# RWKV mixing and a squared-ReLU FFN on one core: steps moved at four places of a hand-written order

## The chip, the cores and the metric

One Trainium2 chip, one of its cores. The metric is the device time of one launch in microseconds (us), as the median of several runs. Five engines work side by side: PE (TensorE, matrix products), DVE (VectorE), ACT (ScalarE), POOL (GpSimd) and SP (SyncE, here only an issuer of transfers). Each runs its own list of instructions in order and waits by semaphores for what the others write. Matrix products land in PSUM, which has eight banks; operands lie in SBUF.

## The reference

An RWKV time mixing in four batches, eight heads of 48 and 768 time steps feeds a feed-forward block of width 384 and hidden width 2048. All inputs and the output are fp32.

```python
for t in range(S):                       # per batch and head
    y[t]  = r[t] @ (state + (u * k[t])^T v[t])
    state = w^T * state + k[t]^T v[t]
x   = y of all heads side by side        # 3072 x 384
out = square(max(x @ w_in, 0)) @ w_out   # 384 -> 2048 -> 384
```

## The kernel before, in words

**Tiling.** Time is cut into chunks of 128 steps. A unit is one chunk of one batch, 128 rows of x; there are 24, numbered in the order in which they are worked. Inside a chunk the recurrence becomes matrix products. r and k are scaled by decay factors (`rh`, `kh`), transposed, and multiplied to scores (`A`), which a triangular mask cuts (`Bm`). Y is the product of masked scores and v, plus the state's part from the second chunk of a batch on. The term of u is a vector: P0 = r times k, P1 = P0 times u, du = its sum over a head, dv = du times v. The state goes on by `U` (k times v), `ts` (U plus state) and `S` (times decay). Units 0 to 3 are *paired*: two chunks of a batch are loaded together with the time steps de-interleaved, so that even steps are unit 2q and odd ones unit 2q+1. They have steps of their own (`lp`, `TK`, `TR`, `Ap`, `Bp`, `YD`, `YI`, `UP`).

**The FFN** works on groups of units: groups 0 and 1 are units 0 and 1, group 2 is units 2 and 3, then two units each (group 4 is units 6 and 7, group 8 is units 14 and 15), and the last two groups are one unit each. `F1.g.s` is piece s of x times w_in for group g, into one PSUM bank: for a group of one unit four pieces of 12 matmuls of 128 columns, for a group of two eight pieces of 6 matmuls of 256 columns. `re` takes the ReLU out of the bank, `sq` squares it, `F2.i.q` is a quarter of the second product for unit i, `os` copies it out and `out` sends it.

**What sets the order.** The string `ORDER` is a table written by hand, one entry for each step, `name.arguments:engine/slots`, with engines A (ACT), D (DVE), G (POOL), P (PE) and S (SP). Each engine runs its steps in the table's order. The slots name the buffers, for PE's steps the PSUM banks; a step that writes a buffer waits for the last reader of what was in it. The dictionary `HELD` says which buffers a step takes.

The steps that the prediction names, with their lines in the kernel before:

- Loads, on SP: `ld.v.16` (L322) brings v of unit 16, which `vb.16` (a copy to bf16, L252 on ACT and L254 on DVE) reads. W_in comes in four parts (`V`), w_out in four (`W`), both issued on POOL.
- `kh` (L338), `rh` (L341), `P0` (L344), `P1` (L348): products of two SBUF tiles, some on DVE, some on POOL. kh.8 and kh.10 are on POOL, kh.11, P0.8, rh.4 and kh.5 on DVE. `du` is L351, `dv` L356.
- `T` (L399, on PE) transposes r and k of a unit into a bank, `Tc` copies that to SBUF. `XB` does the same by a DMA transpose.
- `Ap` (L385) and `A` (L412): scores. `Bp.q.a.h` (L393) and `Bm.i.h` (L420): masks, on DVE, each out of one bank; a is the parity of the time step, h that of the head.
- `YD.0`: Y of units 0 and 1, 36 matmuls. Four bring in dv by an identity (L429), 32 take the masked scores of both a and both h (L438). `YI` adds the state's part (L449). `Y` (L460, L462) is that of the other units.
- `UP` (L472), `U` (L482); `S0` (L496), `ts` (L499), `S` (L502).
- `xs` (L493 on DVE; a copy at L252 or L254 for units 0 to 3) takes Y out of its bank. Then `X` (L507, transposes on PE) and `xTc` (copy into xT) bring x into the form that F1 (L523) reads, or `xX` (L514) does it by one DMA transpose issued on SP. xTc.14 and xX.15 fill the two halves of the xT that F1.8.7, the first piece of group 8, reads.
- `re` (L533 on ACT, L535 on DVE), `sq` (L540 on ACT, L542 on DVE), `F2` (L551).
- `Z.n` (L583): matmuls of the identity whose result nobody reads; Z.7 is four instructions (one of 512 columns, three of 128) behind UP.0.

Behind Z.7 PE does Ap.1.0, YD.0, YI.1, UP.1, X.0, Ap.1.1, X.1, F1.0.3, F1.1.3 and F1.0.0. F1.0.0 uses the bank of UP.1, which ts.3 empties. F1.4.1 and F1.4.7 are the first two pieces of group 4; F1.4.7 takes the bank of U.7, which ts.7 empties. F1.2.4, F1.2.7 and F1.2.5 are the first three of group 2; F1.2.5 follows F1.1.2 in its bank. F2.1.1 takes the bank of A.4, which the masks of unit 4 empty.

Of the kernel before, what the change touches and what calls it, by code (L numbers as in the profile page):

```python
# [26 lines left out]
lp.v.1:S/1 bc:P/3 P0.1:G/0 Wk.0:A/4 rh.1:D/0 ld.r.5:S/4 Wt.0:A/5 bu:P/6 kh.0:D/1 V.3:G WLcol:A P0.0:D/1 Wk.1:A/7  # L27
rh.0:D/1 TR.0:P/0 ld.k.4:S/4 V.0:G kh.1:D/0 ub:A V.1:G TK.0:P/3 rh.3:D/2 rh.2:D/3 RC.0:A/0 KC.0:A/1 ld.r.4:S/5 P1.0:G
TR.1:P/2 vb.0:A/0 vb.1:A/1 kh.2:D/3 kh.3:D/2 Z.2:P/6 Ap.0.1:P/7/5 Ap.0.0:P/4/0 V.2:G P1.1:D TK.1:P/3 ld.k.5:S/5
du.0:D/0 dv.0:G RC.1:A/2 du.1:D/1 dv.1:G Bp.0.1.1:D/0 UP.0:P/6/5 Bp.0.1.0:D/1 Bp.0.0.1:D/2 KC.1:A/3 vb.3:A/2 WLm:G  # L30
Z.7:P/2 Ap.1.0:P/7/2 vb.2:A/3 Bp.0.0.0:D/3 P0.2:G/2 S0.0:D YD.0:P/0/3 ld.v.4:S/4 P1.2:G ts.1:D/1 xs.0:A/0 YI.1:P
Bp.1.0.1:D/4 UP.1:P/4/6 Bp.1.0.0:D/6 X.0:P/5 xs.1:A/1 xTc.0:D/0 S0.2:D Ap.1.1:P/2/0 X.1:P/3 F1.0.3:P/7 ts.3:D/0
xTc.1:A/1 F1.1.3:P/5 P0.3:G/3 P1.3:G du.2:D/2 re.0.3:D/0 F1.0.0:P/6 Bp.1.1.1:D/5 dv.2:G Wt.2:A re.0.0:A/1 W.1:G
du.3:D/3 ld.v.5:S/5 Wk.2:A F1.1.0:P/4 F1.1.1:P/3 dv.3:G re.1.0:A/2 F1.0.1:P/0 rh.5:G/4 re.1.3:A/3 Bp.1.1.0:D/7
YD.1:P/1/7 YI.3:P sq.1.3:A/0 re.0.1:A/4 W.2:G xs.3:D/2 xs.2:A/3 kh.4:D/5 re.1.1:A/5 sq.1.0:D/1 ld.k.6:S/6 W.3:G
F1.0.2:P/6 X.2:P/4 rh.4:D/5 sq.0.0:A/2 X.3:P/2 F1.1.2:P/5 W.0:G re.0.2:D/3 xTc.3:A/0 sq.0.3:A/3 xTc.2:D/0 re.1.2:A/2
P0.4:D/4 T.4:P/0 Tc.4:D/4 F1.2.4:P/1 F1.2.7:P/4 sq.1.2:D/4 F1.2.5:P/5 re.2.4:D/1 re.2.7:A/0 ld.r.6:S/6 sq.0.2:A/5
# [9 lines left out]
F2.2.3:P/4 ld.r.11:S/2 ts.6:D/1 F2.2.1:P/4 sq.3.3:D/17 P0.9:G/3 sq.3.0:A/18 ld.r.10:S/3 F2.2.0:P/4 sq.3.6:A/19  # L47
F1.3.7:P/0 os.2:D/3 du.6:D/2 A.7:P/5/6 A.6:P/1/2 ld.k.11:S/2 re.3.7:A/2 vb.7:G/7 F1.3.5:P/4 Bm.7.1:D/0 sq.3.2:A/20
rh.8:G/2 F2.4.0:P/0 ld.k.10:S/3 Bm.7.0:D/1 Bm.6.0:D/2 Bm.6.1:D/3 sq.3.7:A/21 rh.9:G/1 S.3:G F2.4.1:P/0 re.3.5:D/1
ld.v.8:S/0 XB.9:S/0 P1.9:D dv.6:G out.2:S F2.4.3:P/0 rh.11:G/3 F2.5.0:P/6 ld.v.9:S/1 P0.8:D/4 sq.3.4:A/22 Y.6:P/5  # L50
rh.10:G/5 ld.r.13:S/5 sq.3.5:A/23 F2.5.3:P/6 xs.6:D/1 Y.7:P/4 X.6:P/5 kh.8:G/2 F2.5.1:P/6 xs.7:D/2 xTc.6:A/2 kh.11:D/3
X.7:P/4 U.7:P/5 kh.10:G/5 F2.4.2:P/0 xTc.7:A/2 ts.7:D/0 XB.11:S/2 vb.8:A/0 F1.4.1:P/4 os.4:A/4 S.7:D F1.4.7:P/5
re.4.1:A/3 P0.10:D/1 du.9:D/3 XB.8:S/3 U.8:P/0 F2.5.2:P/6 re.4.7:A/4 vb.9:G/1 S.6:D F1.4.3:P/4 os.5:A/5 XB.10:S/4
P1.8:D re.4.3:D/0 F1.4.4:P/5 F1.4.0:P/6 re.4.4:A/2 rh.13:D/4 ld.k.13:S/4 F1.4.2:P/4 ts.8:D/0 ld.v.11:S/2 re.4.0:A/5
# [17 lines left out]
re.6.4:A/2 xs.12:D/2 xX.12:S/2 F2.11.0:P/2 os.9:D/1 sq.6.4:A/21 P0.16:G/0 XB.17:S/3 ts.13:D/1 Y.13:P/1 kh.16:D/5  # L72
F2.10.3:P/6 rh.16:G/5 F2.10.2:P/6 xs.13:D/3 out.5:S du.15:D/4 ld.k.18:S/4 F2.10.0:P/6 P1.16:G ld.r.21:S/3 A.15:P/7/5
A.14:P/0/3 ld.r.19:S/2 Bm.15.0:D/5 dv.15:G F2.11.1:P/2 ld.r.18:S/5 Bm.15.1:D/7 S.13:G X.13:P/7 F2.11.3:P/2 xTc.13:A/2
Bm.14.0:D/4 Y.15:P/5 vb.14:G/7 du.14:D/0 F1.7.3:P/1 ld.v.16:S/1 kh.19:G/0 xs.15:D/4 xX.15:S/0 F1.7.2:P/7 re.7.3:A/0
Bm.14.1:D/6 F1.7.6:P/0 out.9:S out.6:S os.8:D/3 re.7.2:A/1 ld.r.20:S/4 sq.7.3:D/17 Y.14:P/5 re.7.6:A/3 P0.21:G/3
dv.14:D du.17:D/2 F1.7.1:P/1 XB.16:S/2 os.10:A/4 F1.7.4:P/4 S.12:G xs.14:D/0 F1.7.5:P/7 ld.k.20:S/5 rh.19:G/0 U.15:P/0
F1.7.7:P/6 re.7.5:A/4 ld.v.17:S/0 ts.15:D/1 X.14:P/3 S.15:G F1.7.0:P/5 re.7.7:A/5 xTc.14:D/0 P0.19:D/2 sq.7.2:A/20
# [47 lines left out]
def kernel(  # L126
# [89 lines left out]
    identity = const.tile([128, 128], BF16, name="identity")  # L216
# [39 lines left out]
    class Do:  # L256
# [168 lines left out]
        def YD(e, q):  # L425
# [180 lines left out]
    def dv_of(i):  # L606
        return dvb[slot[f"dv{i}"]].bitcast(BF16)[:, 0 : H // 2].rearrange("p h d -> p (h d)").rearrange("p (h d) -> p h d", h=H)
# [5 lines left out]
    for step in ORDER.split():  # L613
# [4 lines left out]
        x = 2 * at[0] if at and isinstance(at[0], int) else 0  # L618
# [37 lines left out]
```

## Time and profile before

| what | us |
|---|---|
| median of 3 runs | 170.55 |
| lowest and highest run | 170.48, 170.65 |
| the profiled execution | 170.80 |
| its span, first to last instruction | 169.1 |

The clock that PE was granted is 1.00 over the span. All rows and times of the trace come from the one profiled execution; its times count from the start of the span. A row of the trace shows start, duration, engine, line, operation and tiles (out<-in), then shape and count. "x6" is six instructions together, from the first one's start to the last one's end. What stands in square brackets is idle time ahead of the row and the operation that ended it. PEld is PE's loading of weights, beside its matmuls. SPq is SP's issuing of DMAs. A row of the page's queues has packets, MB and the share of the DMA engines; q8 and q14 carry instructions, q0 the transfers that POOL issues, q1 those of SP and ACT.

### The profile page before, as it was taken

Reading aid. Unit: us, or ns where it says so; the run is one execution under the profiler, and the core shown is the slowest. Engines: PE = TensorE matmul, PEld = TensorE weight load, DVE = VectorE, ACT = ScalarE, POOL = GpSimd, SP = SyncE. Lnnn points to the kernel's source line nnn. Section 1 sums busy time; section 2 is a strip of 40 time slices with the busy share of each in tenths; the row PEclk is TensorE's granted clock in tenths of the full one; section 3 lists DMA queues with packets and bytes.
Section 4 is the critical chain, followed back from the end, with each engine's and each line's share of the span. In section 5 each row is a group of like instructions: output and inputs, shape, how many; then the busy total and the mean of one; then the engine's idle time right before and its main releaser. Section 6 shows DMA issues by size and latency. Waiting matters only on the chain.

```text
span 169.1 us, 4580 instructions
## 1 busy us (share of the span) xinstructions
PE 161.0 (95%) x1814; PEld 122.5 (72%) x1814; DVE 137.4 (81%) x253; ACT 100.6 (60%) x189; POOL 101.3 (60%) x125
## 2 busy tenths in 40 slices
PE   4998989999997999999999999999999999999993
PEld 1686878668765776888766878766888676898762
DVE  5699769987899999989998998998779975955400
ACT  4696596851771878349782467952099393254731
POOL 6799861295399318996699988399627760300000
DMA  5999999994999899899986999995939751330032
GB/s 135 323 237 192 217 212 203 180 211 88 194 211 170 177 190 222 194 199 188 227 123 134 223 174 214 219 186 144 179 70 202 204 134 25 103 88 0 6 140 93
DMA packets 97785, 28.02 MB, mean 166 GB/s; under 512 B 92530, under 2 KB 97524, under 8 KB 97764
## 3 DMA queue, kind: packets, MB, share of 16 engines
q1 hardware_dynamic: 93872, 22.42, 67.7%
q0 software_dynamic: 3008, 4.13, 12.4%
q10 hardware_dynamic: 884, 1.18, 2.3%
q8 instruction: 14, 0.23, 0.6%
q14 instruction: 7, 0.06, 0.1%
HBM read 20.45 MB, written 4.72 MB: 149 GB/s over the span
## 4 chain that ended last, share of the span: by engine, by line
PE 82%; DVE 8%; DMA 3%; issue 2%; SPq 2%; ACT 1%; DVEq 0%
PE bank L523 36%; PE bank L551 34%; PE bank L412 3%; DMA ldk<-in_k_dram 3%; PE bank L462 2%; SPq L326 2%; PE bank L460 2%; DVE Bm L393 2%; PE bank L482 2%; PE bank L565 2%; PE bank L507 1%; DVE Bm L420 1%; DVE du L351 1%; DVE P L348 1%; DVE P L344 1%
## 5 line engine op out<-in xcount | busy, mean ns | idle before, releaser
L523 PE MATMUL bank<-xT,W 128*128 128x256 bf16 (+1 forms) x672 | 70.2, 257 | 1.3 <-DVE xT L254 0.6
L551 PE MATMUL bank<-W,hq 128*128 128x384 bf16 x368 | 68.6, 326 | 0.0
L523 PEld LDWEIGHTS <-W 128*128 128x128 bf16 x672 | 56.8, 98 | 9.7 <-DVE xT L254 1.2
L533 ACT ACTIVATE hr<-bank 128x512 bf16<-128x512 f32 x67 | 38.9, 595 | 38.2 <-PE bank L523 29.8
L551 PEld LDWEIGHTS <-hq 128*128 128x128 bf16 x368 | 33.8, 97 | 18.5
L540 ACT ACTIVATE hq<-hr 128x512 bf16<-128x512 bf16 x70 | 41.0, 626 | 4.7 <-DVE hr L535 4.1
L420 DVE TENSOR_TENSOR Bm<-bank,maskJT 128x512 bf16<-128x512 f32 x40 | 25.6, 682 | 2.7 <-PE bank L412 2.7
L535 DVE TENSOR_SCALAR hr<-bank 128x512 bf16<-128x512 f32 x29 | 19.8, 686 | 6.7 <-PE bank L523 4.3
L348 POOL TENSOR_TENSOR P<-P,ub 128x384 f32<-128x384 f32 x15 | 16.0, 1070 | 13.2 <-DVE P L344 12.8
L356 POOL TENSOR_TENSOR dv<-ldv,du 128x384 f32<-128x384 f32 (+1 forms) x18 | 15.5, 872 | 13.4 <-DVE du L351 8.3
L341 POOL TENSOR_TENSOR rk<-ldr,Wt 128x384 bf16<-128x384 f32 x15 | 16.4, 1101 | 0.1
L542 DVE TENSOR_TENSOR hq<-hr 128x512 bf16<-128x512 bf16 x26 | 13.0, 513 | 2.0 <-ACT hr L533 1.8
L344 POOL TENSOR_TENSOR P<-ldr,ldk 128x384 f32<-128x384 f32 x13 | 13.3, 1021 | 1.5 <-DMA ldk<-in_k_dram 1.2
L502 POOL TENSOR_TENSOR S0W<-ts,WLm 128x384 bf16<-128x384 f32 x10 | 10.9, 1091 | 4.2 <-DVE ts L499 3.4
L338 POOL TENSOR_TENSOR rk<-ldk,Wk 128x384 bf16<-128x384 f32 x12 | 12.3, 1033 | 1.4 <-DMA ldk<-in_k_dram 1.4
L351 DVE TENSOR_REDUCE du<-P 128x8 f32<-128x384 f32 x24 | 12.9, 542 | 0.0
L493 DVE TENSOR_TENSOR xs<-bank,dv 128x384 bf16<-128x384 f32 x20 | 11.0, 551 | 2.3 <-POOL dv L356 0.7
L254 DVE COPY os<-bank 128x384 f32<-128x384 f32 x11 | 6.1, 551 | 6.5 <-PE bank L551 6.4
L252 ACT COPY xT<-bank 128x384 bf16<-128x384 bf16 x8 | 3.7, 480 | 10.8 <-PE bank L507 10.8
L499 DVE TENSOR_TENSOR ts<-bank,S0W 128x384 f32<-128x384 f32 x16 | 8.8, 549 | 1.1 <-POOL S0W L502 0.8
L462 PE MATMUL bank<-vb,Bm 128*128 128x48 bf16 x160 | 9.5, 184 | 0.0
L252 ACT COPY os<-bank 128x384 f32<-128x384 f32 (+2 forms) x14 | 6.3, 459 | 4.5 <-PE bank L551 2.5
(81 smaller groups left out, 175.0 us busy)
## 6 DMA issues: line engine op xcount, KB each, us to landing
ldr<-in_r_dram SPq DMA_DIRECT2D x20, 192.0 KB, 3.5
ldk<-in_k_dram SPq DMA_DIRECT2D x20, 192.0 KB, 4.0
ldv<-in_v_dram SPq DMA_DIRECT2D x20, 192.0 KB, 3.6
out_dram<-os SPq DMA_DIRECT2D x9, 192.0 KB, 2.3
W<-in_moe_w_in_dram POOLq DMA_DIRECT2D x4, 384.0 KB, 9.7
W<-in_moe_w_out_dram POOLq DMA_DIRECT2D x4, 384.0 KB, 7.4
out_dram<-os ACTq DMA_DIRECT2D x5, 192.0 KB, 3.9
out_dram<-os POOLq DMA_DIRECT2D x5, 192.0 KB, 3.7
```

The source lines that it names most:

```text
L341: e.tensor_mul(rk[slot[f"rk{i}"]][:, 0, :, 0:D], loaded("r", i), Do.factor("t", i % 2 if i < PAIRED else 2))
L344: e.tensor_mul(P0b[slot[f"P{i}"]], loaded("r", i), loaded("k", i))
L348: e.tensor_mul(t, t, bank("bu")[:, 0 : H * D].rearrange("p (h d) -> p h d", h=H) if i in EARLY_U else ub)
L351: e.tensor_reduce(dub[slot[f"dv{i}"]], P0b[slot[f"P{i}"]], axis=mybir.AxisListType.X, op=ALU.add)
L356: e.tensor_mul(dv_of(i) if i < PAIRED else dvb[slot[f"dv{i}"]], loaded("v", i), t)
L420: e.tensor_mul(Bmb[slot[f"Bm{i}{h}"]], heads(bank(f"bA{i}{h}"), 128), mask_b)
L523: e.matmul(hp[:, fi, :], W1[f // 4][:, c, 256 * (f // 2 % 2) : 256 * (f // 2 % 2 + 1)].rearrange("p (m j) -> p j m", j=2)[:, f % 2, :], xt ...
L533: e.activation(hr, hp, AF.Relu)
L535: e.tensor_scalar_max(hr, hp, 0.0)
L540: e.activation(hq, hr, AF.Square)
L542: e.tensor_mul(hq, hr, hr)
L551: e.matmul(bank(f"bO{i}")[:, 0:d_model], hqb[slot[f"hq{g},{f // m}"]][:, at : at + L], W2[q][:, f % 4, :], start=(seen[i] == 1 and f % 4 = ...
```

## The change

It touches four places of the table and adds one function. No matmul is added or dropped, and POOL's steps keep their order.

1. *The start.* YD.0 becomes YE.0.1 and YE.0.0. YE.0.1 has the four identity matmuls and the 16 of head parity 1, and stands behind UP.0, ahead of Z.7; YE.0.0 has the 16 of head parity 0, behind Z.7. Ap.1.0 now stands behind YE.0.0. On DVE Bp.0.0.1 goes ahead of Bp.0.1.0, and xTc.0 ahead of Bp.1.0.0. The banks of YE, Z.7, Ap.1.0, Ap.1.1, F1.0.3, F1.1.3, F1.0.1 and YD.1 are given anew.
2. *Group 2.* On DVE xTc.2 goes ahead of sq.1.0, rh.4 and re.0.2, on ACT xTc.3 ahead of sq.0.0. On PE F1.2.4 goes ahead of T.4.
3. *Group 4.* On DVE P0.8 goes behind xs.6 and xs.7.
4. *Group 8.* On SP xX.15 goes ahead of ld.v.16.

```diff
-    Y=["bY{0}"], YD=["bY{x}", "bY{y}"], xs=["xs{0}"], U=["bU{0}"], UP=["bU{x}", "bU{y}"],
+    Y=["bY{0}"], YD=["bY{x}", "bY{y}"], YE=["bY{x}", "bY{y}"], xs=["xs{0}"], U=["bU{0}"], UP=["bU{x}", "bU{y}"],
...
+        def YE(e, q, h):
+            y = [heads(bank(f"bY{2 * q + x}"), 2 * D) for x in range(2)]
+            if h:
+                for a in range(2):
+                    for x in range(2):
+                        e.matmul(
+                            y[x][Do.half(a)], identity[Do.half(x), Do.half(x)],
+                            dv_of(2 * q + a)[Do.half(x)].rearrange("p (a e) d -> p a (e d)", e=2),
+                            start=True, stop=False, skip_group_check=True,
+                        )
+            for hc in range(HP):
+                for a in range(2):
+                    for x in range(2):
+                        e.matmul(
+                            y[x][:, hc, D * h : D * (h + 1)],
+                            Bmb[slot[f"Bm{q}{a}{h}"]][Do.half(x), hc, :],
+                            vbb[slot[f"vb{2 * q + a}"]][Do.half(x), 2 * hc + h, :],
+                            start=False, stop=True, skip_group_check=True,
+                        )
...
-du.0:D/0 dv.0:G RC.1:A/2 du.1:D/1 dv.1:G Bp.0.1.1:D/0 UP.0:P/6/5 Bp.0.1.0:D/1 Bp.0.0.1:D/2 KC.1:A/3 vb.3:A/2 WLm:G
+du.0:D/0 dv.0:G RC.1:A/2 du.1:D/1 dv.1:G Bp.0.1.1:D/0 UP.0:P/6/5 Bp.0.0.1:D/2 YE.0.1:P/0/2 Bp.0.1.0:D/1 KC.1:A/3
```

Where the four places now stand is read from each engine's list of instructions, below at three of them. Lines of the changed kernel behind the new function are 20 higher.

DVE at group 2, before. The names are: xs_122 is x of unit 3, rk_80 k and r of unit 4, hq_137 the square of F1.1.0, hr_133 the ReLU of F1.0.2, xT_0_127 the xT of group 2, P_86 is P0.4.

```order
L254 CAST xs_122<-bank_181 128x384
L338 TENSOR_TENSOR rk_80<-ldk_69,Wk 128x8x48
L542 TENSOR_TENSOR hq_137<-hr_132 128x512
L341 TENSOR_TENSOR rk_80<-ldr_65,Wt 128x8x48
L535 TENSOR_SCALAR hr_133<-bank_180 128x512
L254 COPY xT_0_127<-bank_178 128x3x128
L344 TENSOR_TENSOR P_86<-ldr_65,ldk_69 128x384
```

The same place of DVE in the changed kernel:

```order
L254 CAST xs_122<-bank_176 128x384
L338 TENSOR_TENSOR rk_80<-ldk_69,Wk 128x8x48
L254 COPY xT_0_127<-bank_178 128x3x128
L562 TENSOR_TENSOR hq_137<-hr_132 128x512
L341 TENSOR_TENSOR rk_80<-ldr_65,Wt 128x8x48
L555 TENSOR_SCALAR hr_133<-bank_180 128x512
L344 TENSOR_TENSOR P_86<-ldr_65,ldk_69 128x384
```

The copy xTc.2 has moved up past three instructions, a square, a product and a ReLU; the others keep their order.

DVE at group 4, the difference from before to changed. P_85 is P1.9, the two xs are xs.6 and xs.7, P_86 is P0.8, rk_78 is kh.11.

```order
 L348 TENSOR_TENSOR P_85<-P_85,ub 128x384
+L513 TENSOR_TENSOR xs_121<-bank_179,dv_94 128x384
+L513 TENSOR_TENSOR xs_122<-bank_178,dv_93 128x384
 L344 TENSOR_TENSOR P_86<-ldr_63,ldk_67 128x384
-L493 TENSOR_TENSOR xs_121<-bank_179,dv_94 128x384
-L493 TENSOR_TENSOR xs_122<-bank_178,dv_93 128x384
 L338 TENSOR_TENSOR rk_78<-ldk_68,Wk 128x8x48
```

The product P0.8 stands behind the two instructions that it was ahead of, and directly ahead of kh.11.

SP at group 8, the difference. The transpose is xX.15, the load of v ld.v.16; the loads of k and r around them are those of units 18 to 21.

```order
 L322 DMA ldk_69<-in_k_dram 128x8x48
 L322 DMA ldr_64<-in_r_dram 128x8x48 x2
 L322 DMA ldr_65<-in_r_dram 128x8x48
+L534 DMA_TRANSPOSE xT_0_127<-xs_124 128x3x128
 L322 DMA ldv_71<-in_v_dram 128x8x48
-L514 DMA_TRANSPOSE xT_0_127<-xs_124 128x3x128
```

The transpose and the load have changed places; nothing else of SP's list moves.

More of the change, by code (lines that the diff above doesn't have):

```diff
@@ L29 @@
 TR.1:P/2 vb.0:A/0 vb.1:A/1 kh.2:D/3 kh.3:D/2 Z.2:P/6 Ap.0.1:P/7/5 Ap.0.0:P/4/0 V.2:G P1.1:D TK.1:P/3 ld.k.5:S/5
-du.0:D/0 dv.0:G RC.1:A/2 du.1:D/1 dv.1:G Bp.0.1.1:D/0 UP.0:P/6/5 Bp.0.1.0:D/1 Bp.0.0.1:D/2 KC.1:A/3 vb.3:A/2 WLm:G
[L31 to L37, printed above, removed]
+du.0:D/0 dv.0:G RC.1:A/2 du.1:D/1 dv.1:G Bp.0.1.1:D/0 UP.0:P/6/5 Bp.0.0.1:D/2 YE.0.1:P/0/2 Bp.0.1.0:D/1 KC.1:A/3
+vb.3:A/2 WLm:G Z.7:P/7 vb.2:A/3 Bp.0.0.0:D/3 YE.0.0:P/0/2 Ap.1.0:P/7/3 P0.2:G/2 S0.0:D ld.v.4:S/4 P1.2:G ts.1:D/1
+xs.0:A/0 YI.1:P Bp.1.0.1:D/4 UP.1:P/4/6 X.0:P/5 xs.1:A/1 xTc.0:D/0 Bp.1.0.0:D/6 S0.2:D Ap.1.1:P/0/2 X.1:P/3 F1.0.3:P/5
+ts.3:D/0 xTc.1:A/1 F1.1.3:P/7 P0.3:G/3 P1.3:G du.2:D/2 re.0.3:D/0 F1.0.0:P/6 Bp.1.1.1:D/5 dv.2:G Wt.2:A re.0.0:A/1
+W.1:G du.3:D/3 ld.v.5:S/5 Wk.2:A F1.1.0:P/4 F1.1.1:P/3 dv.3:G re.1.0:A/2 F1.0.1:P/5 rh.5:G/4 re.1.3:A/3 Bp.1.1.0:D/7
+YD.1:P/1/2 YI.3:P sq.1.3:A/0 re.0.1:A/4 W.2:G xs.3:D/2 xs.2:A/3 kh.4:D/5 re.1.1:A/5 ld.k.6:S/6 W.3:G F1.0.2:P/6
+X.2:P/4 X.3:P/2 xTc.3:A/0 sq.0.0:A/2 xTc.2:D/0 sq.1.0:D/1 rh.4:D/5 F1.1.2:P/5 W.0:G re.0.2:D/3 sq.0.3:A/3 re.1.2:A/2
+P0.4:D/4 F1.2.4:P/1 T.4:P/0 Tc.4:D/4 F1.2.7:P/4 sq.1.2:D/4 F1.2.5:P/5 re.2.4:D/1 re.2.7:A/0 ld.r.6:S/6 sq.0.2:A/5
 F1.2.1:P/0 re.2.5:D/2 re.2.1:A/3 sq.2.5:D/6 sq.0.1:D/7 F1.2.0:P/6 kh.5:D/4 F1.2.2:P/4 sq.2.1:A/8 F1.2.6:P/5 re.2.2:A/2
@@ L49 @@
 rh.8:G/2 F2.4.0:P/0 ld.k.10:S/3 Bm.7.0:D/1 Bm.6.0:D/2 Bm.6.1:D/3 sq.3.7:A/21 rh.9:G/1 S.3:G F2.4.1:P/0 re.3.5:D/1
-ld.v.8:S/0 XB.9:S/0 P1.9:D dv.6:G out.2:S F2.4.3:P/0 rh.11:G/3 F2.5.0:P/6 ld.v.9:S/1 P0.8:D/4 sq.3.4:A/22 Y.6:P/5
-rh.10:G/5 ld.r.13:S/5 sq.3.5:A/23 F2.5.3:P/6 xs.6:D/1 Y.7:P/4 X.6:P/5 kh.8:G/2 F2.5.1:P/6 xs.7:D/2 xTc.6:A/2 kh.11:D/3
+ld.v.8:S/0 XB.9:S/0 P1.9:D dv.6:G out.2:S F2.4.3:P/0 rh.11:G/3 F2.5.0:P/6 ld.v.9:S/1 sq.3.4:A/22 Y.6:P/5 rh.10:G/5
+ld.r.13:S/5 sq.3.5:A/23 F2.5.3:P/6 xs.6:D/1 Y.7:P/4 X.6:P/5 kh.8:G/2 F2.5.1:P/6 xs.7:D/2 P0.8:D/4 xTc.6:A/2 kh.11:D/3
 X.7:P/4 U.7:P/5 kh.10:G/5 F2.4.2:P/0 xTc.7:A/2 ts.7:D/0 XB.11:S/2 vb.8:A/0 F1.4.1:P/4 os.4:A/4 S.7:D F1.4.7:P/5
@@ L74 @@
 A.14:P/0/3 ld.r.19:S/2 Bm.15.0:D/5 dv.15:G F2.11.1:P/2 ld.r.18:S/5 Bm.15.1:D/7 S.13:G X.13:P/7 F2.11.3:P/2 xTc.13:A/2
-Bm.14.0:D/4 Y.15:P/5 vb.14:G/7 du.14:D/0 F1.7.3:P/1 ld.v.16:S/1 kh.19:G/0 xs.15:D/4 xX.15:S/0 F1.7.2:P/7 re.7.3:A/0
+Bm.14.0:D/4 Y.15:P/5 vb.14:G/7 du.14:D/0 F1.7.3:P/1 kh.19:G/0 xs.15:D/4 xX.15:S/0 ld.v.16:S/1 F1.7.2:P/7 re.7.3:A/0
 Bm.14.1:D/6 F1.7.6:P/0 out.9:S out.6:S os.8:D/3 re.7.2:A/1 ld.r.20:S/4 sq.7.3:D/17 Y.14:P/5 re.7.6:A/3 P0.21:G/3
```

## The prediction

> **What bounds the kernel now.** I read the busy shares first, then the chain of waits in order of time, then busy time by stretch.
>
> ```profile
> PE 161.0 (95%) x1814; PEld 122.5 (72%) x1814; DVE 137.4 (81%) x253; ACT 100.6 (60%) x189; POOL 101.3 (60%) x125
> ```
>
> PE is busy for 95% of the span, so only two things can change the time: PE's work, and the places where PE stands still. The change adds no matmul and drops none (36 of the split Y for 36 of the old one). So I look for the stops. The chain shows three of them behind the first 14 us:
>
> ```profile
> 18.32 0.41 issue
> 18.73 2.58 PE bank L523 x43
> ...
> 24.76 0.36 DVE xT L254
> 25.16 4.76 PE bank L523 x42
> ...
> 53.98 0.48 DVE xs L493
> 54.50 0.34 PE bank L507 x3
> ```
>
> A fourth is in the rows under D. Their price is the start of the row behind the stop, less the start due after the matmul before it. Matmuls of 128 columns follow each other by 0.056 us (the row of 43: 2.58 less one matmul's 0.22, over 42), those of 256 columns by 0.109. The prices are 0.56 at 18.7 (stop 1), 0.63 at 25.2 (stop 2), 1.32 at 54.5 (stop 3) and 0.43 at 101.4 (stop 4), 2.94 us in all. How much a stretch would pass on shows in the busy times (columns: PE, PEld, DVE, ACT, POOL, each with its count):
>
> ```profile
> 22.40:33.40 11.00, 10.53 (x122) 8.61 (x120) 10.77 (x22) 8.54 (x17) 2.71 (x4) 1.00 1.11 200
> 56.30:99.00 42.70, 42.70 (x476) 33.11 (x474) 40.55 (x70) 27.76 (x53) 33.05 (x35) 1.00 1.00 188
> 101.40:166.00 64.60, 64.60 (x679) 49.28 (x680) 46.55 (x83) 36.16 (x70) 28.21 (x33) 1.00 0.56 125
> ```
>
> Between 22.4 and 33.4 DVE is full (10.77 of 11.00). From 56.3 to 99 and from 101.4 on PE never stands still, and DVE has 2 and 18 us to spare: a lead gained there is carried, if what feeds PE moves along.
>
> **The change, term by term.**
>
> *A, the start (Y of pair 0 in two parts, x of unit 0 ahead of a mask, new banks).*
>
> ```profile
> 11.14 1.61 POOL L356 TENSOR_TENSOR dv<-ldv,du 128x384 bf16<-128x384 f32 x2 [0.38 <-DVE du L351]
> 14.95 1.28 DVE L393 TENSOR_TENSOR Bm<-bank,maskP 128x512 bf16<-128x512 f32 x2
> 16.14 0.35 DVE L254 COPY xT<-bank 128x384 bf16<-128x384 bf16 x1
> 16.54 1.78 PE L523 MATMUL bank<-xT,W 128*128 128x128 bf16 x29 [0.17 <-DVE xT L254]
> 16.99 0.56 DVE L499 TENSOR_TENSOR ts<-bank,S0W 128x384 f32<-128x384 f32 x1
> q8 instruction: 14, 0.23, 0.6%
> q0 software_dynamic: 476, 0.47, 92.7%
> q8 instruction: 1, 0.02, 2.0%
> ```
>
> YE.0.1 now starts once dv.1 is there (POOL, 12.76), and its work leaves the path. But Ap.1.0 goes behind YE.0.0, so that X.0 comes hardly earlier. What helps is xTc.0: it no longer waits for the second mask (0.60 of the 1.28). It runs from about 15.69 to 16.04, and F1.0.3 starts at about 16.09 instead of 16.54. F1.0.0 gets little of that: its bank comes from UP.1 and is freed by ts.3, which stays behind the delayed mask and ends near 17.69 (before 17.55). It starts near 17.75 instead of 17.88 (16.54 plus 24 matmuls). Then comes stop 1. It falls inside F1.0.0, behind 12+12+5 of the 29 matmuls; the chain calls it "issue", and the program has no wait there. I read it as PE's own instructions arriving late. The page's q8 moved 14 packets of 16 KB, and 3,628 loads and matmuls make about 259 a packet. 128 pairs back from the stop lies the last matmul of UP.0, where the packet before would begin. Between 16 and 19 us one packet came, while q0 with the weights held 93% of the DMA engines. Neither that place in the program nor the traffic before it changes, so the packet should come at the same moment, and all of A's lead waits for it. **A: 0**, between +0.05 (nothing of it stays hidden but the jitter of the packet, by the 0.06 of one matmul) and -0.13.
>
> The Trainium skill (Runtime: NRT & Kernel Launch, Instruction fetch mechanics) says that instructions stream in blocks of 256 and that crossing a block is mostly hidden. The block size agrees with the 259 here. That it is hidden does not, with 0.56 us lost. By the rule A would be worth 0.13.
>
> *B, x of units 2 and 3 earlier, F1.2.4 ahead of T.4.*
>
> ```profile
> 22.95 0.51 PE L507 MATMUL bank<-identity,xs 128*128 128x128 bf16 x6
> 23.96 0.73 PE L399 MATMUL bank<-identity,rk 128*128 128x128 bf16 x8
> 23.36 0.42 DVE L542 TENSOR_TENSOR hq<-hr 128x512 bf16<-128x512 bf16 x1
> 23.79 0.49 ACT L252 COPY xT<-bank 128x384 bf16<-128x384 bf16 x1
> 28.75 0.55 DVE L338 TENSOR_TENSOR rk<-ldk,Wk 128x384 bf16<-128x384 f32 x1
> 32.12 1.29 DVE L420 TENSOR_TENSOR Bm<-bank,maskJT 128x512 bf16<-128x512 f32 x2
> ```
>
> xTc.2 takes the place of sq.1.0 at 23.36 and ends at 23.71. xTc.3 starts when X.3 is out (23.46) and ends at 23.98 after its 0.49. F1.2.4 starts at 24.04, as PE comes free (23.96), and T.4 follows at 24.70. F1.2.7 starts at 25.15 instead of 25.82: 0.67 ahead. sq.0.0, rh.4 and re.0.2 each start about 0.3 later, behind the copies. The first that PE wants is re.1.2, for the bank of F1.2.5 at 25.80; it moves back with them to about 25.6 (an estimate). A loss would need T.4 out behind DVE's turn for Tc.4, which follows the same instructions as before. But DVE executes the same instructions without a gap: kh.5 (28.75 to 29.30) can come only 0.08 earlier, T.5 needs it, and the lead is 0.48 there. At 33.4 the two masks of unit 4 end (32.12 plus 1.29); F2.1.1 takes their bank 0.06 later. DVE's idle time up to there is 0.23, of which the reordering adds another 0.06 at most. **B: -0.29**, between -0.10 (only part of that idle goes) and -0.63 (the whole stop).
>
> *C, P0.8 behind xs.6 and xs.7.*
>
> ```profile
> 53.13 0.21 PE L462 MATMUL bank<-vb,Bm 128*128 128x48 bf16 x2
> 53.52 2.27 POOL L338 TENSOR_TENSOR rk<-ldk,Wk 128x384 bf16<-128x384 f32 x2
> 53.90 1.01 DVE L493 TENSOR_TENSOR xs<-bank,dv 128x384 bf16<-128x384 f32 x2
> 54.83 1.38 DVE L338 TENSOR_TENSOR rk<-ldk,Wk 128x384 bf16<-128x384 f32 x1
> 56.13 0.54 DVE L499 TENSOR_TENSOR ts<-bank,S0W 128x384 f32<-128x384 f32 x1
> 56.32 1.47 PE L523 MATMUL bank<-xT,W 128*128 128x256 bf16 x12
> ```
>
> P0.8 ended at 53.98 (where the chain's xs begins) and held xs.6 up. In the times of before, xs.6 starts at 52.63 and xs.7 once Y.7 is out (53.34); X.6 starts at 53.23 and stop 3 is gone: F1.4.1 could start at 55.04 instead of 56.32. What is late next is DVE. The same product, L338, takes 0.55 at 28.75 and 1.38 at 54.83, where POOL's L338 runs beside it and DVE ends 0.42 behind POOL (55.79, 56.21): products with both inputs in SBUF take turns on the two engines. So P0.8, now ready at 53.84, gives way to kh.8 on POOL (to 54.53) and ends at 54.95; kh.10 then runs to 55.80 and kh.11 on DVE to 56.22. Thus ts.7 ends at 56.68, exactly as before, and F1.4.7 writes the bank that ts.7 reads. F1.4.7 started at 56.97 (56.32 plus 6 times 0.109) and now starts at 56.73, behind a new stop of about 1.0 us. **C: -0.24**, between +0.2 (POOL runs both kh in a row, and kh.11 ends 0.42 later) and -1.27 (ts.7 early enough). I take the value that the order of turns gives.
>
> A rule of the Trainium skill speaks against this edit (SBUF — State Buffer, Who interferes with whom): a DVE instruction with two SBUF inputs contends with a GpSimd one that reads SBUF, and the one that comes second blocks. The 1.38 agrees. Without such a rule C would be -1.27.
>
> *D, xX.15 ahead of ld.v.16.*
>
> ```profile
> 95.16 0.55 DVE L493 TENSOR_TENSOR xs<-bank,dv 128x384 bf16<-128x384 f32 x1
> 95.61 0.70 SPq L322 DMA_DIRECT2D ldv<-in_v_dram  x1
> 96.41 1.50 SPq L514 DMA_TRANSPOSE xT<-xs  x1
> 100.31 0.82 PE L523 MATMUL bank<-xT,W 128*128 128x256 bf16 x6
> 100.51 0.36 DVE L254 COPY xT<-bank 128x384 bf16<-128x384 bf16 x1
> 101.40 0.27 PE L523 MATMUL bank<-xT,W 128*128 128x256 bf16 x1 [0.27 <-ACT hq L540]
> 102.20 0.50 ACT L252 CAST vb<-ldv 128x384 bf16<-128x384 f32 x1
> DMA to landing us min/median/max: 4.9/4.9/4.9
> ```
>
> xX.15 issued at 96.41 and landed 4.9 later, at 101.3, where PE goes on. xs.15 is there at 95.71. Issued at 95.78 it lands at 100.6, ahead of the 100.97 at which F1.8.7 is due; xTc.14, the other half, ended at 100.87 (100.51 plus 0.36). F1.8.7 is due 0.109 behind the last of the six matmuls from 100.31. The row names ACT as what ended the wait; F1.8.7 reads nothing of ACT, and its xT landed 0.1 earlier. ld.v.16 issues 1.5 later, near 97.3; its reader vb.16 starts at 102.20. **D: -0.43**, between 0 and that.
>
> *The sum.* The profiled execution took 170.80 us (span 169.1). 170.80 - 0.29 - 0.24 - 0.43 = 169.84. It lay 0.25 above the median of the runs, so the forecast for that median is 170.55 - 0.96, or **169.6 us**. P0.8's consumer and the swapped banks cost nothing: P1.8 is the seventh DVE instruction behind it, and each new bank is read out before its next writer on PE, but for the one named in A.
>
> **Rivals.**
>
> 1. *All stops go and the lead is carried* (0.13 + 0.63 + 1.27 + 0.43): 168.1. For it: PE never idles after 56. Against: DVE is full up to 33.4, and turns with POOL fix ts.7. This one holds the skill's hidden blocks too. Chance 0.12.
> 2. *The leads are given back.* DVE's full stretches and its turns with POOL set when xs.14 is ready, which feeds X.14 just ahead of F1.8.7. If DVE and POOL do not move along with PE, B and C end there, and xTc.14 (0.1 before F1.8.7 was due) can take D. Between -0.43 and 0, so 170.1 to 170.55; it decides if xs.14 ends no earlier than now. Chance 0.25.
> 3. *Slower.* PE's next block is asked for where UP.0 ends. Before, Z.7 followed freely; now YE.0.1 follows and waits for dv.1 to 12.76. If the request leaves only behind that wait, the packet can fall behind another quarter of the weights: q0 moved 0.47 MB in those 3 us, so 0.39 MB is 2.5 us (an estimate). With B whole that gives 170.55 + 2.5 - 0.63 - 0.24 - 0.43 = 171.75. It decides once PE resumes past 19.9. Chance 0.08.
>
> That the program does not do as written is excluded by the instruction rows shown above.
>
> **How the numbers follow.** The forecast has 0.55, with 169.2 to 170.1 as its own range. About 0.2% (0.34 us) is what a measurement here can tell from no change. Faster by more: 0.55 + 0.12 + a fifth of rival 2, which is 0.72; within: the rest of rival 2, 0.20; slower: rival 3, 0.08. The range takes in most of rivals 1 and 2: 168.3 to 170.6.
>
> **What would show it.** A: PE still stops inside F1.0.0 and goes on at 18.7. B: F1.2.4 at 24.0, the masks of unit 4 done about 0.3 earlier. C: no wait ahead of X.6, P0.8 at 1.1 us and a new stop of about 1 us ahead of F1.4.7, ended by ts. D: no wait at F1.8.7. A first stop that is shorter, or an F1.4.7 that does not wait, would prove me wrong.

## The result and the profile after

The changed kernel takes 169.62 us (median of ten runs, 169.46 to 170.87). The kernel before, run beside it, has 171.1 (ten runs, 170.48 to 172.51); the ratio is 0.9926, 95% interval 0.9903 to 0.995. Times and ratios here and below leave out the few executions that took over 1.5% longer than the fastest of their kernel. The forecast was 169.6. It was made for the three runs of before with a median of 170.55, and that the medians meet so closely is partly luck: the two profiled executions, 170.80 and 169.49 us, differ by 1.31, where the sum of the terms was 0.96. So the terms are what has to be looked at.

The busy shares of the changed kernel: PE does the same work (161.0 us, 1814 matmuls) in a span of 167.8.

```profile
PE 161.0 (96%) x1814; PEld 122.9 (73%) x1814; DVE 134.9 (80%) x253; ACT 100.9 (60%) x189; POOL 100.7 (60%) x125
```

The chain of waits of the changed kernel, in order of time (start, duration, what):

```profile
17.31 0.57 DVE ts L519
17.92 0.44 PE bank L543 x5
18.36 0.39 issue
18.75 0.58 PE bank L543 x7
...
53.41 0.76 DVE P L344
54.17 0.23 issue
54.41 1.36 DVE rk L338
55.76 0.48 DVE ts L519
56.24 0.04 issue
56.28 0.81 PE bank L543 x6
```

Stop 1 is where it was, behind the fifth matmul of F1.0.0, and ends at 18.75 instead of 18.73. Stops 2 and 4 are gone. In place of stop 3 a new one stands ahead of F1.4.7, at 56.28, and ts.7 ends it. A small one is new at the start: F1.0.0 begins at 17.92, 0.25 later than F1.1.3 would let it, because its bank waits for ts.3 (the first row).

How far PE is ahead is read best from the start of the same step in two traces. Starts in the kernel before, and what the others add to them (us; below zero is earlier):

| step | before | changed | A alone | B alone | C alone | D alone |
|---|---|---|---|---|---|---|
| F1.0.3 | 16.54 | -0.27 | -0.05 | +0.16 | +0.14 | +0.14 |
| F1.1.0, behind stop 1 | 19.14 | +0.02 | 0.00 | +0.01 | 0.00 | 0.00 |
| F1.2.7, behind stop 2 | 25.83 | -0.69 | 0.00 | -0.69 | 0.00 | 0.00 |
| F2.4.0 | 49.19 | -0.44 | 0.00 | -0.49 | 0.00 | 0.00 |
| F2.6.3, behind stop 3 | 66.84 | -0.69 | -0.01 | -0.50 | -0.26 | -0.01 |
| F1.7.5 | 98.47 | -0.69 | -0.01 | -0.51 | -0.26 | -0.01 |
| F1.8.6, behind stop 4 | 102.05 | -1.31 | -0.04 | -0.61 | -0.17 | -0.63 |
| F1.13.3, near the end | 158.20 | -1.31 | -0.04 | -0.61 | -0.15 | -0.56 |

In the changed kernel the four parts bring +0.02, -0.46, -0.25 and -0.62. A lead won at one place stays until the next stop, and in the changed kernel nothing is lost any more behind 102 us (D alone loses 0.08 on the way). B, C and D alone start as the kernel before does, so their +0.14 to +0.16 at F1.0.3 are a difference between executions and not an effect.

### The profile page after: what moved, and what is told of

It is laid out like the page before. It is cut to its first block, busy times and chain, and to the rows that moved or that the text cites. A ratio compares the mean times of both kernels' runs of the same rounds, so it can differ in the third digit from the quotient of the medians.

```text
span 167.8 us, 4580 instructions
## 1 busy us (share of the span) xinstructions
PE 161.0 (96%) x1814; PEld 122.9 (73%) x1814; DVE 134.9 (80%) x253; ACT 100.9 (60%) x189; POOL 100.7 (60%) x125
## 3 DMA queue, kind: packets, MB, share of 16 engines
q10 hardware_dynamic: 884, 1.18, 2.3%
## 4 chain that ended last, share of the span: by engine, by line
PE 77%; DVE 9%; ACT 4%; issue 3%; DMA 3%; SPq 2%; ACTq 0%
PE bank L571 34%; PE bank L543 32%; PE bank L412 3%; DMA ldk<-in_k_dram 3%; PE bank L482 2%; ACT hr L553 2%; SPq L326 2%; PE bank L480 2%; PE bank L585 2%; PE bank L502 2%; DVE hr L555 1%; ACT hq L560 1%; DVE Bm L393 1%; DVE rk L338 1%; DVE hq L562 1%
## 5 line engine op out<-in xcount | busy, mean ns | idle before, releaser
L562 DVE TENSOR_TENSOR hq<-hr 128x512 bf16<-128x512 bf16 x26 | 12.1, 477 | 2.0 <-ACT hr L553 1.8
```

Source lines behind the costliest of these rows:

```text
L562: e.tensor_mul(hq, hr, hr)
```

## The experiments

### The four parts, each alone on the kernel before

The edits are those of the change, one part at a time: A is the start with YE; B, C and D are these lines of the table (in full steps; what isn't named stays):

```diff
 B
-... sq.1.0:D/1 ... rh.4:D/5 sq.0.0:A/2 ... re.0.2:D/3 xTc.3:A/0 sq.0.3:A/3 xTc.2:D/0 ... T.4:P/0 Tc.4:D/4 F1.2.4:P/1
+... xTc.3:A/0 sq.0.0:A/2 xTc.2:D/0 sq.1.0:D/1 rh.4:D/5 ... re.0.2:D/3 sq.0.3:A/3 ... F1.2.4:P/1 T.4:P/0 Tc.4:D/4
 C
-P0.8:D/4 ... xs.6:D/1 ... xs.7:D/2
+xs.6:D/1 ... xs.7:D/2 P0.8:D/4
 D
-ld.v.16:S/1 kh.19:G/0 xs.15:D/4 xX.15:S/0
+kh.19:G/0 xs.15:D/4 xX.15:S/0 ld.v.16:S/1
```

> The kernel before with part A alone (Y of the first pair in two parts, x of unit 0 ahead of a mask, new banks). My theory, that PE's own instructions arrive late inside F1.0.0 and that A does not move the arrival: PE is ahead by about 0.2 us at the start of F1.0.3, stops inside F1.0.0 behind its fifth matmul, goes on at 18.7 us as before, and the time is that of before within 0.05 us. Rival, that A is worth something by itself: F1.1.0 starts 0.1 to 0.2 us earlier and the time falls by as much.

**Measured:** ratio to before 1.0003 (0.9985 to 1.002). In its profile PE reached the fifth matmul of F1.0.0 at 18.36, 0.25 later than before, and went on at 18.73 all the same. At F1.0.3 it was 0.05 ahead and not 0.2. Against B, C and D alone, with the start of before, it was 0.2 ahead. But no lead reached stop 1: F1.0.0 waited 0.25 for its bank, which ts.3 empties, and started at 18.14, 0.1 later than with B, C or D. So what stop 1 took away here was lateness. My theory, that A does not move the end of the stop, stands.

> The kernel before with part B alone (x of units 2 and 3 ahead of other work, F1.2.4 ahead of T.4). The trace of the changed kernel has PE 0.44 us ahead behind unit 4's masks, not the 0.29 forecast. My theory, that each part is worth its own stop: 0.44 us less. If the stop ahead of X.14 (0.18 us) depends on who comes first, DVE's sq.7.3 or POOL's P0.21, a DVE that is 0.44 us earlier comes first, that stop goes too, and the time falls by 0.62. Rival, that the later stops take the lead back: no gain, with a longer wait ahead of F1.4.1 or F1.8.7.

**Measured:** ratio 0.9965 (0.9945 to 0.9984), 0.61 us in the profile. My theory holds up to 98 us, with 0.5. What comes behind is not what I expected: the stop ahead of X.14 is gone, but its 0.18 is not simply added. F1.8.7 still waits, 0.52 us, for xX.15, which in this kernel landed at 100.65 (before: 101.26). F1.8.7 starts 0.14 behind that landing in both, and so whatever PE had won up to there is replaced by what the landing gives, here 0.61.

> The kernel before with part C alone (P0.8 behind xs.6 and xs.7). My theory, that the turns of DVE and POOL leave ts.7 where it was: no wait ahead of X.6, P0.8 at about 1.1 us, a wait of about 1.0 us ahead of F1.4.7 that ts.7 ends, and 0.25 us less. Rival: 1.3 us less, if ts.7 comes earlier when C stands alone.

**Measured:** ratio 0.9977 (0.9965 to 0.999). No wait ahead of X.6, and PE's rows of this kernel have the new stop:

```profile
55.03 0.82 PE L523 MATMUL bank<-xT,W 128*128 128x256 bf16 x6
56.72 0.81 PE L523 MATMUL bank<-xT,W 128*128 128x256 bf16 x6 [0.87 <-DVE ts L499]
```

F1.4.1 starts at 55.03 (1.29 earlier than before), F1.4.7 only at 56.72, behind a stop of 1.03 (1.69 less the six matmuls of F1.4.1, 0.66). 0.26 is kept. The rival's 1.3 is out. Behind 98 us xX.15 landed at 101.09 and left 0.17.

> The kernel before with part D alone (xX.15 ahead of ld.v.16). My theory: the wait at F1.8.7 goes, the stop of 0.18 us ahead of X.14 stays since DVE is no earlier there, and the time falls by 0.43 us. Rival, that D itself also ends the stop ahead of X.14, by moving the load of v away from POOL's P0.21: 0.61 us less.

**Measured:** ratio 0.9972 (0.9955 to 0.9989); 0.63 in the profile at F1.8.6. Both theories are off: the 0.61 of the rival is there, but not by its mechanism, since the stop ahead of X.14 is missing with A alone, B alone and C alone too. DVE and POOL in the kernel before, around xs.14 (the last DVE row), first DVE:

```profile
96.69 1.18 DVE L542 TENSOR_TENSOR hq<-hr 128x512 bf16<-128x512 bf16 x1
97.79 1.36 DVE L356 TENSOR_TENSOR dv<-ldv,du 128x384 f32<-128x384 f32 x1
99.07 0.54 DVE L351 TENSOR_REDUCE du<-P 128x8 f32<-128x384 f32 x1
99.53 0.54 DVE L493 TENSOR_TENSOR xs<-bank,dv 128x384 bf16<-128x384 f32 x1
```

POOL beside it, P0.21 and S.12:

```profile
96.59 1.00 POOL L344 TENSOR_TENSOR P<-ldr,ldk 128x384 f32<-128x384 f32 x1 [0.21 <-DMA ldr<-in_r_dram]
97.55 1.18 POOL L502 TENSOR_TENSOR S0W<-ts,WLm 128x384 bf16<-128x384 f32 x1
```

With D alone, DVE:

```profile
96.67 0.42 DVE L542 TENSOR_TENSOR hq<-hr 128x512 bf16<-128x512 bf16 x1
97.00 1.36 DVE L356 TENSOR_TENSOR dv<-ldv,du 128x384 f32<-128x384 f32 x1
98.28 0.54 DVE L351 TENSOR_REDUCE du<-P 128x8 f32<-128x384 f32 x1
98.75 0.54 DVE L493 TENSOR_TENSOR xs<-bank,dv 128x384 bf16<-128x384 f32 x1
```

and POOL:

```profile
96.83 1.12 POOL L344 TENSOR_TENSOR P<-ldr,ldk 128x384 f32<-128x384 f32 x1 [0.46 <-DMA ldr<-in_r_dram]
```

DVE's square (sq.7.3) starts within 0.02 of the same time in both. Before, POOL's P0.21 had started 0.1 ahead of it, when r of unit 21 landed, and the square took 1.18 instead of 0.42. With D alone r landed 0.24 later, the square came first, xs.14 is 0.79 earlier and X.14 does not wait. The same holds with A alone, where SP's order is that of before (P0.21 at 96.76, the square 0.42). With C alone POOL was first again (P0.21 at 96.19, the square at 96.42 with 1.04), but r had landed so early that POOL did not wait for it; xs.14 started at 99.12, 0.41 earlier than before, and X.14 did not wait either. So the 0.18 ahead of X.14 hung on when one load landed, within a few tenths of a us, and it was in the one profile that I had. Without it F1.8.7 is due 0.18 sooner, and a wait that ends at a landing is longer by as much (0.59 with A alone). D is worth 0.61, the 0.43 that I read off plus the 0.18 ahead of it.

### C's stop: the bank, or the order on DVE

```diff
 e2_bank (on the changed kernel)
-X.7:P/4 U.7:P/5
+X.7:P/4 U.7:P/3
 e2_P08 (on the changed kernel)
-xs.7:D/2 P0.8:D/4 xTc.6:A/2 kh.11:D/3 ... ts.7:D/0 XB.11:S/2
+xs.7:D/2 xTc.6:A/2 kh.11:D/3 ... ts.7:D/0 P0.8:D/4 XB.11:S/2
```

> The changed kernel with U.7 in bank 3 instead of 5, so that F1.4.7 no longer waits for ts.7. DVE's work stays where it is. My theory, that DVE's list is what C left as the bound: the wait of 1.03 us ahead of F1.4.7 goes, but F1.4.2 (its bank waits for re.4.3 on DVE, 0.35 us to spare) and F1.4.5 (its bank waits for ts.8 on DVE, 0.24 to spare) stop PE a few us later, and about 0.25 us of the 1.03 is kept. Rival, that the bank alone was the matter: all of it is kept, 1.0 us less than the changed kernel.

**Measured:** 169.7 us (four runs), ratio to before 0.9918 (0.9887 to 0.9949), not to be told from the changed kernel. PE's rows:

```profile
54.70 1.47 PE L543 MATMUL bank<-xT,W 128*128 128x256 bf16 x12
...
56.83 2.13 PE L543 MATMUL bank<-xT,W 128*128 128x256 bf16 x18
59.44 0.81 PE L543 MATMUL bank<-xT,W 128*128 128x256 bf16 x6 [0.49 <-DVE hr L555]
```

F1.4.1 and F1.4.7 follow each other; three pieces later F1.4.2 stops for 0.65, and DVE's re.4.3 ends it. Against the changed kernel PE goes from 0.10 behind (49 us; it had waited 0.43 at 30.0 for a quarter of w_out) to 0.17 ahead (67 us): 0.27 is kept of 1.03. DVE's list was the bound, as expected. At 100 us F1.8.7 waits again, 0.22, and the profile ends 0.05 behind that of the changed kernel. xX.15 was issued at 95.38 here and at 95.27 there, so SP had not come along with PE's lead; that its landing ended this wait is likely (in the four profiles that record it, it landed 4.4 to 4.9 us behind its issue, here that would be 99.8 to 100.2), but the trace has no record of the landing.

> The changed kernel with P0.8 one place pair further back on DVE, behind kh.11 and ts.7. My theory of the turns: kh.11 now meets kh.8 on POOL and takes about 1.07 us instead of P0.8, ts.7 reads PSUM and takes 0.55 beside kh.10, so ts.7 ends at 55.0 instead of 56.23 and the wait ahead of F1.4.7 goes; DVE has its two products and ts.7 done about 0.3 us earlier. PE then keeps 0.3 to 0.6 us. Rivals: all 1.03 is kept; or nothing, if kh.11 and ts.7 take turns with both of POOL's products and ts.7 ends at 56.2 all the same.

**Measured:** 169.22 us (four runs, 168.84 to 169.45), ratio to before 0.9893 (0.9866 to 0.992). DVE of this kernel, from kh.11 on:

```profile
53.64 1.07 DVE L338 TENSOR_TENSOR rk<-ldk,Wk 128x384 bf16<-128x384 f32 x1
54.63 0.55 DVE L519 TENSOR_TENSOR ts<-bank,S0W 128x384 f32<-128x384 f32 x1
55.10 0.89 DVE L344 TENSOR_TENSOR P<-ldr,ldk 128x384 f32<-128x384 f32 x1
```

POOL beside it, kh.8 and kh.10:

```profile
53.30 2.27 POOL L338 TENSOR_TENSOR rk<-ldk,Wk 128x384 bf16<-128x384 f32 x2
```

The turns came as forecast: kh.11 in P0.8's place is the one of 1.07, and ts.7, with one input in PSUM, takes its 0.55 in the middle of kh.10. PE's F1.4.1 and F1.4.7 are one row:

```profile
54.82 1.47 PE L543 MATMUL bank<-xT,W 128*128 128x256 bf16 x12
```

PE goes from 0.23 behind the changed kernel (49 us; the reason is under B below) to 0.64 ahead (67 us): 0.87 is kept, more than my 0.3 to 0.6. In the two kernels below that have this edit too, 0.73 and 0.54 are kept, and F1.4.2 waits 0.19 and 0.39 for re.4.3. I had left out that DVE is done with its three steps earlier too: re.4.3, which stopped F1.4.2 with the other bank, ends at 58.92 instead of 59.39 there.

### Stop 1: does it follow the count of instructions, and what sets its end

```diff
 e2_noZ7 (on the changed kernel)
-Z.7:P/7 vb.2:A/3
+vb.2:A/3
 e4_V12_late (on the changed kernel)
-ub:A V.1:G TK.0:P/3 ... Ap.0.0:P/4/0 V.2:G P1.1:D ... P1.2:G ts.1:D/1
+ub:A TK.0:P/3 ... Ap.0.0:P/4/0 P1.1:D ... P1.2:G V.1:G V.2:G ts.1:D/1
```

> The changed kernel without Z.7, the four matmuls of the identity behind UP.0 that nobody reads. My theory of stop 1, that PE's instructions 128 matmuls behind the last one of UP.0 arrive at a fixed moment: the stop moves four matmuls further, to behind the ninth of F1.0.0, PE goes on at 18.7 us as before, and all that follows is 0.22 us earlier (4 times 0.056), of which 0.2 us is left at the end. Rival, that the stop belongs to what F1.0.0 does and not to the count of instructions: it stays behind the fifth matmul, and nothing is gained.

**Measured:** 169.48 us (nine runs), ratio to before 0.9945 (0.9903 to 0.9987). The chain of this kernel:

```profile
18.21 0.66 PE bank L543 x9
18.87 0.12 issue
18.99 0.36 PE bank L543 x3
```

The stop has moved by exactly four matmuls, to behind the ninth, so it belongs to a place in the list of instructions and not to F1.0.0. The fixed moment failed in this execution: by the trace's record of q8 the packet started at 16.79 instead of 16.37, PE went on at 18.99, and nothing was gained.

> The changed kernel with the second and third quarter of w_in (V.1 and V.2, 0.39 MB each) issued behind P1.2 on POOL, at about 15.7 us instead of 8.3 and 10.0. It is to tell what sets the moment at which PE's instruction packet comes (16.1 to 16.8 us in all profiles so far). If the traffic on the queue of the weights holds it up: q0 is empty from 15 to 17 us, the packet starts at 15.5 us or earlier, PE goes on inside F1.0.0 as soon as ts.3 lets it, and stop 1 is gone. If the packet is only asked for late: it starts at 16.3 to 16.5 us all the same and PE stops until 18.7. Either way the whole is not faster, since F1.0.1 and F1.0.2 then wait for their weights and POOL issues them in the middle of P0.3 and P1.3: up to 2 us more.

**Measured:** 172.64 us, ratio 1.01 (1.0068 to 1.0131); F1.1.1 waits 2.1 us for its weights, F1.0.2 another 0.9. The packet started at 15.83, 0.54 earlier, between the two expectations. PE came to F1.0.0 only at 18.48 and ran through it, so the length of stop 1 was not tried. The queues of this kernel between 15 and 18.8 us:

```profile
q1 hardware_dynamic: 3484, 0.66, 91.8%
q0 software_dynamic: 23, 0.02, 10.2%
q8 instruction: 1, 0.02, 1.9%
```

The weights left the engines, but the loads of SP filled them. That traffic has a part in the moment the packet comes is likely, but it is not settled.

### Together

```diff
 e3_vb4 (on the changed kernel)
-vb.4:G/4 Bm.4.1:D/0 ... dv.4:G Y.4:P/0
+Bm.4.1:D/0 ... dv.4:G vb.4:G/4 Y.4:P/0
 e3_P08_vb4: this and the edit of e2_P08
 e3_P08_vb4_noZ7: these and the edit of e2_noZ7
```

> The changed kernel with vb.4 (v of unit 4 to bf16, on POOL) behind dv.4 instead of as soon as v has landed. My theory of B's size: how much of B's 0.63 us is kept depends on whether DVE's sq.1.2 meets vb.4 (0.65 us long in the profile of before, 0.42 to 0.46 otherwise). With vb.4 moved, sq.1.2 takes 0.42, kh.5 ends in time for T.5, and PE is 0.45 to 0.5 us ahead of before at Y.4. Rival: sq.1.2 is as long as it was, or vb.4 is too late for Y.4 and PE waits there.

**Measured:** 169.71 us, ratio to before 0.9932 (0.9907 to 0.9957), the same as the changed kernel. sq.1.2 takes 0.41 and PE is 0.49 ahead at F2.4.0, as with B alone (there vb.4 happened to come at 30.2, when v landed). In the profile of the changed kernel sq.1.2 had met only the end of vb.4 (0.46), so little was left to gain.

> The changed kernel with P0.8 behind ts.7 and vb.4 behind dv.4. Theory: the two add, 0.87 us of the former wait ahead of F1.4.7 and up to 0.2 at sq.1.2, so 168.6 to 168.8 us, and no stop of more than 0.25 us behind 20 us. Rival: the stop ahead of X.14 comes back, with DVE's sq.7.3 and dv.14 both behind POOL's products, and takes 0.2 to 0.5 of it.

**Measured:** 168.82 us (six runs, 168.71 to 170.64), ratio to before 0.9895 (0.9863 to 0.9926). Span 167.1. The stop ahead of X.14 did not come back, and no stop behind 20 us is longer than 0.22. PE's rows at stop 1:

```profile
17.33 0.85 PE L543 MATMUL bank<-xT,W 128*128 128x128 bf16 x8
18.48 1.01 PE L543 MATMUL bank<-xT,W 128*128 128x128 bf16 x15 [0.30 <-issue]
```

It ends at 18.48 instead of 18.75, and the packet had started 0.25 earlier than in the changed kernel, at 16.12. That part of this profile's lead is luck.

> The same without Z.7. Theory: the stop in F1.0.0 lies behind its ninth matmul, the packet with PE's instructions starts at 16.4 us as in eight of nine profiles so far, PE goes on at 18.7, and the time is 0.2 us less than with Z.7. Rival, that the packet comes later without Z.7 (16.79 in the one profile so far): nothing gained.

**Measured:** 168.85 us (five runs, 168.45 to 169.69), ratio to before 0.9884 (0.986 to 0.9908). In its profile the packet started at 16.37, the stop lies behind the ninth matmul and ends at 18.73, and F1.1.0 starts at 18.91, 0.24 earlier than in the changed kernel, whose packet started at the same moment. That is the 0.22 expected. In the end it is not faster than with Z.7: PE waited 0.33 for a quarter of w_out at 29.6 and 0.39 for re.4.3 at 58.8, and 0.13 ahead of X.14, where POOL's P0.21 started 0.15 ahead of the square again (1.14).

## Why the forecast was right, step by step

**A, forecast 0: the number right, the way to it only in part.** Stop 1 ended at 18.75 (before: 18.73), as forecast. But it had no lead to take away. I had F1.0.0 at 17.75, 0.13 ahead, because ts.3 would end near 17.69. It ended at 17.87, and F1.0.0 started at 17.92, 0.04 later than before: the lead of 0.27 at F1.0.3 was already gone there. F1.0.0 waits 0.21 to 0.25 for ts.3 in all nine profiles with YE. In the six of them that change nothing else ahead of it, it starts at 17.75 to 18.29, in the mean at 18.01, and with B, C and D alone, which have the start of before, at 18.02 to 18.04. So A would likely be worth nothing without stop 1 too, and the 0.13 that rival 1 counts is not seen.

That the end of stop 1 does not follow PE is shown all the same. In eight other profiles with the stop behind the fifth matmul, PE came there between 17.97 and 18.51; it went on between 18.73 and 18.75 in seven of them, and at 18.48 in the one whose packet was 0.25 early. Rival 3 did not come: the packet started at 16.37 although YE.0.1 now stands behind UP.0. UP.0's last matmul started between 12.42 and 13.36 in thirteen profiles, and the packet does not follow it: the earliest but one (12.46) and the latest but one (13.25) had packets at 16.36 and 16.43.

The later packets tell more. Call an edge the place where a packet's instructions begin: stop 1, and every 128 matmuls from there (an estimate from the 14 packets for 3,628 loads and matmuls). In the kernel before, the 13 packets behind that of stop 1 each start between 1.5 us ahead of and 2.2 us behind the moment at which PE passes the edge before theirs. That speaks for a request near that edge, as rival 3 had it. For the packet of stop 1 the edge before is the end of UP.0, and the packet started 2.5 to 3.9 us behind it in the 13 profiles; why so late there stays open.

The place of the stop follows the count of 256 instructions in the Trainium skill (Runtime: NRT & Kernel Launch, Instruction fetch mechanics), as the four matmuls of e2_noZ7 show. What it says besides, that crossing a block is mostly hidden, fails at this one edge, with 0.2 to 0.6 us lost in every profile but that of e4_V12_late, and holds at the twelve later edges of the kernel before, where PE runs on without a gap.

**B, forecast -0.29: mechanism right, size too small** (-0.46 between F1.1.0 and F2.4.0; -0.50 alone). xTc.2, xTc.3 and F1.2.4 came as worked out: F1.2.4 at 24.05, T.4 at 24.70, F1.2.7 at 25.14. The rows of PE in the changed kernel:

```profile
23.32 1.54 PE L543 MATMUL bank<-xT,W 128*128 128x128 bf16 x18
24.70 0.61 PE L399 MATMUL bank<-identity,rk 128*128 128x128 bf16 x8
25.14 2.13 PE L543 MATMUL bank<-xT,W 128*128 128x256 bf16 x18
```

The step that failed is "DVE executes the same instructions without a gap: kh.5 can come only 0.08 earlier". It came 0.22 earlier, with sq.1.2 0.19 shorter. In the kernel before, DVE:

```profile
25.49 0.69 DVE L254 COPY rkT<-bank 128x1024 bf16<-128x1024 bf16 x1
26.09 0.65 DVE L542 TENSOR_TENSOR hq<-hr 128x512 bf16<-128x512 bf16 x1
```

and POOL beside it:

```profile
25.97 0.50 POOL L254 CAST vb<-ldv 128x384 bf16<-128x384 f32 x1 [2.28 <-DMA ldv<-in_v_dram]
```

In the changed kernel DVE's square starts 0.07 later and POOL's copy of v 0.13 earlier:

```profile
26.16 0.46 DVE L562 TENSOR_TENSOR hq<-hr 128x512 bf16<-128x512 bf16 x1
```

The square has both inputs in SBUF and had been held up by the copy. I took DVE's 10.77 of 11.00 us for work, though the same kind of square takes 0.42 in a row that I had quoted (23.36). Part of the full stretch was waiting. Besides that, re.2.6 no longer waits 0.14 for PE. The masks of unit 4 end at 32.87, 0.54 earlier and not 0.3, and F2.1.1 is 0.55 ahead; 0.11 of it goes at F2.3.2 (34.64), which now waits for a square on ACT.

The short square alone is not enough. With A, C and D alone it took 0.51, 0.42 and 0.56, and kh.5 still came at 28.74 to 28.75, because DVE then waited for PE. With C alone:

```profile
27.34 0.69 DVE L535 TENSOR_SCALAR hr<-bank 128x512 bf16<-128x512 f32 x1 [0.23 <-PE bank L523]
```

Nor is PE's lead. In the profile of e2_P08, whose lists up to there are those of the changed kernel, POOL's copy started at 26.07, 0.09 ahead of the square:

```profile
26.16 0.69 DVE L562 TENSOR_TENSOR hq<-hr 128x512 bf16<-128x512 bf16 x1
```

There kh.5 came at 28.76, T.5 waited 0.30 for it, and F2.1.1 was 0.33 ahead, close to the forecast. So at F2.1.1 B is worth about the forecast when the square has to wait out most of the copy, and 0.2 to 0.3 more when it need not; which of the two comes hangs on one landing, that of v.

**C, forecast -0.24: right, -0.25** (-0.26 alone), in the mechanism too. All its rows came: P0.8 1.07 (forecast 1.1), then kh.11 1.36 and ts.7 up to 56.23, which is 56.68 less B's 0.45. The stop of 1.03 stands ahead of F1.4.7, ended by ts. What the row of 1.38 said about turns, and what the Trainium skill says (SBUF — State Buffer, Who interferes with whom), was enough to tell -0.24 from -1.27; e2_P08 shows the same rule from the other side, since there ts.7 is let past.

**D, forecast -0.43: mechanism right, size too small** (-0.62; -0.61 to -0.63 alone). The term had one stop too few: the 0.18 ahead of X.14 was a wait in front of a wait. I had left it out of the four stops. It is gone in the changed kernel for the reason shown with D alone: there sq.7.3 takes 0.42 and dv.14 0.56.

**The rivals.** Rival 2, leads given back, is out by its own sign: xs.14 ends at 97.8 in the changed kernel and at 100.1 before. Leads are given back by another way: with B or C alone F1.8.7 starts 0.14 behind the landing of xX.15 whatever PE had won. With D in the change it is seen no more, save perhaps for the 0.22 of e2_bank. Rival 1 would have needed ts.7 early, which takes the edit of e2_P08, and A's 0.13.

## What to carry to other kernels

Before you call an engine's stretch full, look whether its instructions are as long as elsewhere in the same trace: a square of 0.65 us that takes 0.42 in other rows is 0.23 us of waiting that no idle column shows. It can go by itself, from one execution to the next, and it is worth something only if the engine's next inputs come earlier too. A stop that ends at a landing hides every shorter stop ahead of it, so add those to its price. And where two engines take turns, moving the long product behind the one instruction that others wait for (here ts.7) did more for PE than giving the waiter another bank: 0.54 to 0.87 us in three profiles against 0.27 in one (the intervals of the measured ratios overlap).

## What the runs showed of the hardware

- DVE and POOL products with both inputs in SBUF take turns, and 0.1 us decides who waits: sq.7.3 took 0.42 us when it started 0.16 ahead of POOL's P0.21, and 1.18 when it started 0.10 behind. A copy to bf16 on POOL (0.50) that starts 0.1 ahead makes DVE's square 0.65 to 0.69 instead of 0.42, one that starts 0.3 ahead 0.46. An addition with one input in PSUM (ts.7) keeps its 0.55 beside a POOL product.
- Such meetings differ from profile to profile with the landing of one load, each by about 0.2 us of PE's time (0.18 ahead of X.14; F2.1.1 0.33 or 0.55 ahead); a single profile shows one draw.
- PE went on 2.2 to 2.4 us behind the start of its instruction packet in all twelve profiles that had stop 1, whether the packet started at 16.12 (18.48), 16.37 (18.75) or 16.79 (18.99).
